# Outer products of the backward chain in 64-row tiles over two head groups, with score gradients in two zero-filled column blocks

## The chip, the cores and the metric

The kernel runs on one core of a Trainium2 chip. The metric is the device time of one launch in microseconds (us); three runs of the kernel before took 2824.84, 2825.89 and 2842.98 us, the median is 2825.89. The engines are named as in the profile: PE is TensorE's matrix multiplication and PEld its weight loads, DVE is VectorE, ACT ScalarE, POOL GpSimd, SP the engine that issues most DMAs (SPq its queue).

## The reference, cut to what matters

One layer and all its gradients. The attention part is recurrent: the sequence of 2048 rows is cut into 64 segments of 32, and 8 memory rows, which are the attention's own output at the segment before, stand ahead of each. There are 32 heads of size 128, the model has 512 columns.

```python
for s in range(n_seg):                                    # 64 segments
    xs = x[:, s * seg_len:(s + 1) * seg_len, :].copy()    # 32 rows
    h = jnp.concatenate([mem, xs], axis=1)                # 8 + 32 = 40 rows
    q = jnp.einsum('btd,dhe->bhte', h, Wq)                # k, v alike
    scores = jnp.einsum('bhqe,bhke->bhqk', q, k) * scale  # then masked
    p = _softmax(scores, axis=-1)
    o = jnp.einsum('bhqk,bhke->bhqe', p, v)
    o = jnp.einsum('bhte,hed->btd', o, Wo)
    mem = o[:, :M, :].copy()                              # M = 8
    outs.append(o[:, M:, :])
```

Beside it stands a feed-forward part with a squared ReLU. The kernel returns the output and the gradients of x, mem0, Wq, Wk, Wv, Wo, w1, b1, w2 and b2. The gradient walks the segments from the last to the first, because each segment's memory gradient is needed by the one before it.

## The kernel before

The program has five parts one after the other: the feed-forward part, the forward chain, the gradients of the memory rows ("left" rows), the backward chain, and the weight gradients. The change lies in the backward chain alone, from B_ORDER to the end of its pool block.

The chain has 64 steps, one for each segment, in 16 blocks of SPB = 4. The 32 heads are four groups (HG = 4) of KH = 8. An SBUF tile holds the 32 rows of a segment for the four groups on its 128 partitions, group g on partitions 32 g to 32 g + 31, and the eight heads of a group beside each other in columns. A step works on two halves p of four heads a group. Its operations, by the names in the table of orders:

- o0mm, o1mm project the incoming gradient with Wo (L390), o0ev, o1ev copy it to gON, o0fl, o1fl transpose it (L167), o0te, o1te copy that to gOT on DVE (L435).
- vp0, vp1 form the value gradients: probabilities (PD) times gON, a product over the segment's rows.
- s0, s1 form the gradients of the probabilities in PSUM (L477). d1 to d4, with the half behind them (d10, d41), turn these on DVE into score gradients gS (L585, L589, L592, L595); tu0, tu1 transpose gS in blocks of 32x32 on DVE into gST (L495).
- kp0, kp1 and qp0, qp1 form the key and query gradients from gS and the queries qN, and from gST and the keys kN. A second matmul adds what the left rows contribute (qNL with GL, kNL with gST).
- ve, vl, ke, kl and qe copy these results out of PSUM, on ACT and DVE (the table ENGS says which); vg, kg and qg multiply them with the turned weights into one sum (L505); ra and rb copy that sum out, ta and tb transpose it (L541), Ha and Hb add it over the groups into the gradient of the step that follows (L550).
- ldp, ldq and ldn load P, qN and kN for the following step through POOL's queue; vtr loads its values transposed through SP's; vc and pb, on POOL, build vT and PD from them; ldv and ldk load the left rows' PGD, gOL, GL and qNL once a block through POOL's queue; ldk0 and ldk1 load kNL once a block through SP's. Names that begin with L. are the left rows' own products (L1284), sums and stores.

vp multiplies all 128 rows at once: for each head number k, the four groups' heads are columns of PD, which is zero outside a group's own 32 partitions, so one matmul of 160 columns (L1417) and one of 64 for the left rows (L1419) serve four heads. kp and qp go through the helper outer (L636), which places each group's matmul on its own 32 rows of the array, four side by side: for each head number, four matmuls of the segment's rows and four of the left rows'.

The order of the work is written by hand. B_ORDER has four rows, for the four places of a step in its block; each "+" behind a name says that the operation belongs to a later step than the row's, so a step begins in one row and ends in the next. Every engine takes its instructions strictly in the order in which the rows issue them, and DMA issues stand in the queue of the engine that issues them.

## Time and profile before

| what | value |
|---|---|
| median of three runs | 2825.89 us |
| the profiled execution's own time | 2830.48 us |
| its span | 2828.7 us, mean granted clock 0.984 |
| the backward chain, 1335 to 2260 us of the span | 925 us: PE busy 842.42, DVE 482.19, ACT 337.09, POOL 362.65 |
| matmuls in that stretch | 22,832 |
| outer products of kp and qp (L636, output b_pp) | 8,192, in sets of four |
| value products (L1417 and L1419) | 512 and 512 |

The page gives busy time of each engine, and an idle engine is no loss unless the work waits for it. In this stretch PE is the engine with least idle time. The view of waits says for each engine what ended its idle time; "issue" there means that nothing the profile shows ended it. A timeline row is the start in us, the duration in us, the engine, line, operation, the tile written and the tiles read, the shapes and the number of instructions drawn together; the duration of a matmul is a modelled one and contains its way through the array, so how fast matmuls follow each other is read from start to start.

### The profile page before, as it was taken

To read this page: it belongs to the slowest core of one execution; us is meant where nothing else is said; L and a number is where in the kernel's file an instruction comes from. 1 tells how busy PE (TensorE), PEld (TensorE's weight loads), DVE (VectorE), ACT (ScalarE), POOL (GpSimd) and SP (SyncE) were. 2 spreads that over 40 slices of the span, in tenths; PEclk is the share of its full clock that TensorE was granted. 3 is DMA by queue.
4 is the path that set the end of the run, shared out by engine and by line. 5 is a ranking of instruction groups with operands and counts; after the bars stand their busy time and mean duration, and the time that the engine had idled before them with its cause. 6 is when DMAs were issued, how large, how long until landed. Compare 5 with 4: busy or idle time off the path is not lost.

```text
span 2828.7 us, 116974 instructions
## 1 busy us (share of the span) xinstructions
PE 2654.5 (94%) x52405; PEld 1449.8 (51%) x52405; DVE 1295.7 (46%) x3819; ACT 976.3 (35%) x2266; POOL 658.9 (23%) x1280
## 2 busy tenths in 40 slices
PE   8999999999999998898998999899899899999999
PEld 3445555555555555455555555555555444444444
DVE  4545656666656664444555555555555401000000
ACT  2324444444444445332333333333333301111111
POOL 1000000000000000123344333343334334322221
PEclk9999999999999999999999999999999999999999
DMA  9764689899989988998577877788777799999992
GB/s 250 274 230 154 165 198 219 205 207 225 220 200 228 210 214 210 260 268 221 152 182 200 208 179 179 184 210 193 175 182 194 228 334 228 216 211 207 201 212 66
DMA packets 842008, 586.76 MB, mean 207 GB/s; under 512 B 638033, under 2 KB 729826, under 8 KB 838178
## 3 DMA queue, kind: packets, MB, share of 16 engines
q1 hardware_dynamic: 800802, 457.86, 70.4%
q0 software_dynamic: 40416, 121.16, 14.1%
q8 instruction: 411, 6.73, 1.0%
q14 instruction: 91, 0.75, 0.1%
q10 hardware_dynamic: 288, 0.26, 0.0%
HBM read 184.95 MB, written 248.79 MB: 153 GB/s over the span
## 4 chain that ended last, share of the span: by engine, by line
PE 47%; issue 3%; DVE 1%; ACT 0%; DMA 0%; POOL 0%; SPq 0%; ACTq 0%; POOLq 0%; DVEq 0%
PE ps_gw L1677 20%; PE ps_gR L505 11%; PE ps_proj L390 4%; PE ps_RL L1284 3%; PE b_pp L636 3%; PE b_T L541 2%; PE ps_tr L167 1%; PE ps_sc L477 1%; PE b_pp L1417 1%; DVE gOT L435 1%; PE ps_R L505 1%; ACT R L432 0%; PE b_pp L1419 0%; DMA b_kNL<-S_NL 0%; PE ps_rows L1588 0%
## 5 line engine op out<-in xcount | busy, mean ns | idle before, releaser
L1677 PE MATMUL ps_gw<-gn,HNc 128*128 128x512 bf16 x1920 | 416.5, 379 | 0.0
L1677 PEld LDWEIGHTS <-HNc 128*128 128x128 bf16 x1920 | 187.9, 98 | 223.8
L432 ACT CAST f_N<-ps_proj 128x512 bf16<-128x512 f32 x320 | 184.1, 581 | 194.8 <-PE ps_proj L390 187.7
L1607 ACT CAST wt<-ps_gw 128x512 bf16<-128x512 f32 x128 | 73.8, 589 | 443.1 <-PE ps_gw L1677 369.3
L390 PEld LDWEIGHTS <-X 128*32 128x32 bf16 x5760 | 144.6, 96 | 135.9 <-DVE X L550 19.8
L1590 DVE TENSOR_TENSOR gx<-ps_rows,gb 128x512 f32<-128x512 f32 x16 | 11.1, 691 | 420.5 <-PE ps_rows L1588 420.5
L896 POOL COPY kM<-f_kT 128x256 bf16<-128x256 bf16 x64 | 25.8, 403 | 749.3 <-DVE f_kT L435 564.1
L505 PE MATMUL ps_gR<-Wv,gv 128*32 128x512 bf16 x2048 | 137.2, 390 | 6.5 <-issue 4.5
L1677 PE MATMUL ps_gw<-GOc,gn 128*128 128x512 bf16 x640 | 139.1, 379 | 1.2 <-DVE gm L1523 1.1
L505 PE MATMUL ps_R<-Wo,OT 128*32 128x256 bf16 x4096 | 128.8, 278 | 6.2 <-issue 5.1
L505 PE MATMUL ps_gR<-Wk,gk 128*32 128x512 bf16 (+1 forms) x2048 | 128.5, 371 | 2.6 <-issue 2.4
L1608 POOL DMA_DIRECT2D out_dram<-wt x120 | 65.0, 543 | 275.8 <-ACT wt L1607 262.0
L390 PE MATMUL ps_proj<-Wo,GT 128*32 128x512 bf16 x2048 | 124.4, 384 | 5.1 <-DVE GT L1329 4.5
L432 ACT CAST gON<-ps_proj 128x512 bf16<-128x512 f32 x128 | 75.0, 586 | 154.7 <-PE ps_proj L390 154.7
L390 PE MATMUL ps_proj<-Wq,X 128*32 128x512 bf16 x1920 | 127.7, 384 | 0.6 <-issue 0.6
L505 PE MATMUL ps_gR<-Wq,gq 128*32 128x512 bf16 (+1 forms) x2048 | 119.9, 350 | 6.7 <-issue 6.6
L390 PE MATMUL ps_proj<-Wk,X 128*32 128x512 bf16 x1920 | 124.9, 384 | 1.1 <-issue 0.4
L390 PE MATMUL ps_proj<-Wv,X 128*32 128x512 bf16 x1920 | 121.5, 378 | 0.2 <-issue 0.2
L1365 POOL COPY PD<-b_P 32x320 bf16<-32x320 bf16 x256 | 115.0, 449 | 17.2 <-DMA b_P<-S_A 6.4
L505 PEld LDWEIGHTS <-OT 128*32 128x32 bf16 x4096 | 105.1, 98 | 14.0 <-issue 7.4
L432 ACT CAST gk<-b_pp 128x256 bf16<-128x256 f32 x128 | 48.1, 376 | 163.4 <-PE b_pp L636 161.3
L505 PEld LDWEIGHTS <-gq 128*32 128x32 bf16 x2816 | 75.4, 98 | 54.0 <-issue 18.8
(290 smaller groups left out, 5271.3 us busy)
## 6 DMA issues: line engine op xcount, KB each, us to landing
S_A<-f_N SPq DMA_DIRECT2D x64, 512.0 KB
out_dram<-wt POOLq DMA_DIRECT2D x134, 128.0 KB, 5.2
S_A<-f_N SPq DMA_DIRECT2D x64, 256.0 KB
S_GB<-gv SPq DMA_DIRECT2D x32, 512.0 KB
S_GB<-gk SPq DMA_DIRECT2D x32, 512.0 KB
S_GB<-gq SPq DMA_DIRECT2D x32, 512.0 KB
b_qN<-S_A POOLq DMA_DIRECT2D x63, 256.0 KB, 3.7
b_kN<-S_A POOLq DMA_DIRECT2D x63, 256.0 KB, 4.9
```

The costliest lines, as they stand in the source:

```text
L167: nc.tensor.transpose(ps_ap, in_ap, ident[base:base + k, base:base + k])
L390: nc.tensor.matmul(o, lhsT=hT[:, dc, :], rhs=x, start=(dc == 0), stop=(dc == DC - 1), tile_position=(0, 32 * g))
L432: nc.scalar.copy(out, in_)
L435: nc.vector.tensor_copy(out, in_)
L505: nc.tensor.matmul(R[32 * g:32 * g + 32, 0:(cs.stop - cs.start) * P].rearrange("p (a b) -> p a b", b=P), lhsT=XT(k, g), rhs=x[:, cs, :], s ...
L541: nc.tensor.transpose(st["T", h][:, 0, c * P:(c + 1) * P], st["R4"][:, (2 * h + c) * P:(2 * h + c + 1) * P], identF[:])
L636: nc.tensor.matmul(o, lhsT=N_[32 * g:32 * g + m, kk * P:(kk + 1) * P], rhs=X(kk)[32 * g:32 * g + m], start=(i == 0), stop=(i == len(jobs) ...
L1284: nc.tensor.matmul(ps["R", i][32 * g:32 * g + 32, :].rearrange("p (a b) -> p a b", b=P), lhsT=B_[n][:, k, g, :], rhs=W(g * KH + k), start= ...
L1365: nc.gpsimd.tensor_copy(PD[32 * g:32 * g + 32, g], C["P"][32 * g:32 * g + 32, :, KW - L:KW])
L1607: nc.scalar.copy(wt[:], ps[:])
L1608: eng(dst, wt[:])
L1677: nc.tensor.matmul(ps[:], lhsT=l(rc), rhs=r(rc), start=(n == 0), stop=(n == RC_ALL - 1))
```

## The change

vp, kp and qp get one helper, halves. For each head number it places two matmuls, on rows 0 to 63 and 64 to 127 of the array, side by side. A half holds two head groups, and the moving operand has two blocks of columns, one for each: a block is zero on the 32 partitions of the other group. So the score gradients gS and the probabilities PD now have the shape [half p, block a, head, column], d4 writes both blocks at once by multiplying with PD (whose zeros make the zeros of gS), and the transposition of gS turns both, with zeros. GLD takes the place of GL, in the same two blocks, filled by four loads a block instead of one; kM takes the place of kNL: a tile that is zero except for the 8 memory rows of the step's place in each group, loaded by four small loads a step (ldm) instead of two loads a block. PSUM is laid out anew: a half of vp has a bank, a half of kp and qp a pair of banks. B_ORDER changes in four ways: ldm stands behind ra in each row, ldk0 and ldk1 are gone, in the second row vea and vg0 stand ahead of kp0, and in the third pb stands behind d41.

Per step kp and qp have 64 matmuls instead of 128 and vp 32 instead of 16. A main matmul of kp has 80 columns instead of 40, of the left rows 32 instead of 16; of qp both have 64 instead of 32; of vp 80 instead of 160 and 32 instead of 64.

```diff
@@ -576,7 +576,7 @@
         for c in range(DC):
             nc.tensor.transpose(ps[:, c * P:(c + 1) * P], XT[:, c].rearrange("p j r -> p (j r)"), identF[:])
-    def ds_ops(o, p, n, sc, Pb, gS, sm):
+    def ds_ops(o, p, n, sc, Pb, gS, sm, last=None):
         t, rr = {}, {}
@@ -592,6 +592,9 @@
             nc.vector.tensor_tensor(out=t[0][:], in0=sc3(sc(), n), in1=bc(rr[0], n), op=ALU.subtract)
         def d4():
+            if last is not None:
+                last(t[0])
+                return
             nc.vector.scalar_tensor_tensor(out=gS()[:, HALF[p], KW - n:KW], in0=t[0][:], scalar=scale,
                                            in1=Pb()[:, HALF[p], :], op0=ALU.mult, op1=ALU.mult)
         o["d1%d" % p], o["d2%d" % p], o["d3%d" % p], o["d4%d" % p] = d1, d2, d3, d4
...
-        "L.G3+ L.I3+ s1+++++ kp0+++++ qp0+++++ d11+++++ vea+++++ d21+++++ vg0+++++ vlb+++++ d31+++++ veb+++++ "
+        "L.G3+ L.I3+ s1+++++ vea+++++ vg0+++++ kp0+++++ qp0+++++ d11+++++ d21+++++ vlb+++++ d31+++++ veb+++++ vg1+++++ "
...
     with sb("bq", 1) as bq, sb("bt", 1) as bt, sb("bs", 2) as bs, sb("be", 1) as be, psum("bpp", 1) as bpp, psum("br", 4) as br:
         G4 = {n: bq.tile([P, HG, KH, SPB, SEG], BF16, name="g" + n) for n in "vkq"}
-        gS = bq.tile([P, KH, KW], BF16, name="gS")
-        nc.vector.memset(gS[:], 0.0)
-
-        PD = be.tile([P, HG, KH, L], BF16, name="PD")
-        PGD = be.tile([P, HG, KH, KW], BF16, name="PGD")
+        gS = bq.tile([P, 2, 2, 4, L], BF16, name="gS")
+        PD = be.tile([P, 2, 2, 4, L], BF16, name="PD")
+        PGD = be.tile([P, 2, KH, KW], BF16, name="PGD")
+        GLD = be.tile([P, 2, KH, KW], BF16, name="GLD")
+        kM = be.tile([P, GW], BF16, name="kM")
         nc.vector.memset(PD[:], 0.0)
         nc.vector.memset(PGD[:], 0.0)
+        nc.vector.memset(GLD[:], 0.0)
+        nc.vector.memset(kM[:], 0.0)
...
         def ldv(b, q=pdma):
             for g in range(HG):
-                q(PGD[32 * g:32 * g + 32, g], S_PL[b][32 * g:32 * g + 32])
+                q(PGD[32 * g:32 * g + 32, g % 2], S_PL[b][32 * g:32 * g + 32])
             q(block(b)["gOL"][:], S_GOL[b])
         def ldk(b, q=pdma):
-            q(block(b)["GL"][:, 0], S_GSL[b])
+            for g in range(HG):
+                q(GLD[32 * g:32 * g + 32, g % 2], S_GSL[b][32 * g:32 * g + 32])
             q(block(b)["qNL"][:], S_NL[b][:, 0, :])
...
             def pb():
                 for g in range(HG):
-                    nc.gpsimd.tensor_copy(PD[32 * g:32 * g + 32, g], C["P"][32 * g:32 * g + 32, :, KW - L:KW])
+                    nc.gpsimd.tensor_copy(PD[32 * g:32 * g + 32, :, g % 2],
+                                          C["P"][32 * g:32 * g + 32, :, KW - L:KW].rearrange("p (h k) n -> p h k n", h=2))
             o["pb"] = pb
             o["ldq"] = lambda q=pdma: q(tile_of("qN", [P, GW])[:], rows[:, GW:2 * GW])
             o["ldn"] = lambda q=pdma: q(tile_of("kN", [P, GW])[:], rows[:, 2 * GW:3 * GW])
-            for p in range(2):
-                o["ldk%d" % p] = lambda p=p: dma(B_["kNL"][:, HC[p]], S_NL[b][:, 1, HC[p]]) if j == SPB - 1 else None
+
+            def ldm():
+                for g in range(HG):
+                    dma(kM[32 * g:32 * g + M], S_NL[b][32 * g + M * j:32 * g + M * j + M, 1, :])
+            o["ldm"] = ldm
...
-                ds_ops(o, p, L, lambda p=p: ps["s", p], lambda: C["P"][:, :, KW - L:KW], lambda: gS, bt)
+
+                def d4(t, p=p):
+                    nc.vector.scalar_tensor_tensor(out=gS[:, p], in0=t[:].unsqueeze(1).to_broadcast([P, 2, 4, L]), scalar=scale,
+                                                   in1=PD[:, p], op0=ALU.mult, op1=ALU.mult)
+                ds_ops(o, p, L, lambda p=p: ps["s", p], lambda: C["P"][:, :, KW - L:KW], None, bt, d4)
                 def tu(p=p):
-                    st[p] = bt.tile([P, 4, 2, 32], BF16, name="gST", tag="gST%d" % p)
-                    turn(st[p], gS, p, j)
+                    st[p] = bt.tile([P, 2, 4, 2, 32], BF16, name="gST", tag="gST%d" % p)
+                    x = gS[:, p]
+                    nc.vector.transpose(st[p][:].rearrange("p a k e q -> p (a k e q)"),
+                                        bass.AP(x.tensor, x.offset, [x.ap[0], [L, 8], [M, 2], [1, SEG]]))
                 o["tu%d" % p] = tu
-                def pair(k):
-
-                    return B_["GL"][:, 0, k, :].rearrange("p (a n) -> p a n", a=2)[:, :, lc]
+                def halves(out, k, jobs):
+                    for i, (X, Y, ends) in enumerate(jobs):
+                        for x in range(2):
+                            r, o = slice(64 * x, 64 * x + 64), out(x)
+                            if ends:
+                                o = o[:, :, 0:2 * M].rearrange("p a (e n) -> p a e n", e=2)
+                            nc.tensor.matmul(o, lhsT=X[r, k * P:(k + 1) * P], rhs=Y(k)[r], start=(i == 0),
+                                             stop=(i == len(jobs) - 1), tile_position=(64 * x, 0), skip_group_check=True)
+
+                def ends_of(T_):
+                    return lambda k: T_[:, :, k, :].rearrange("p a (e n) -> p a e n", e=2)[:, :, :, lc]
                 def vp(p=p):
                     for k in range(4 * p, 4 * p + 4):
-                        o = pp("v")[p][:, k % 4 // 2, k % 2 * 256:k % 2 * 256 + 256].rearrange("p (g n) -> p g n", g=HG)
-                        nc.tensor.matmul(o[:, :, 0:L], lhsT=T["gON"][:, k * P:(k + 1) * P], rhs=PD[:, :, k, :],
-                                         start=True, stop=False, skip_group_check=True)
-                        nc.tensor.matmul(o[:, :, 0:2 * M].rearrange("p g (a n) -> p g a n", a=2),
-                                         lhsT=B_["gOL"][:, k * P:(k + 1) * P],
-                                         rhs=PGD[:, :, k, :].rearrange("p g (a n) -> p g a n", a=2)[:, :, :, lc],
-                                         start=False, stop=True, skip_group_check=True)
+                        halves(lambda x: pp("v")[p][:, x, k % 4 * P:k % 4 * P + P].rearrange("p (a n) -> p a n", a=2)[:, :, 0:L], k,
+                               ((T["gON"], lambda k: PD[:, p, :, k % 4, :], False), (B_["gOL"], ends_of(PGD), True)))
                 def kp(p=p):
-                    outer(pp(p), p, ((KW, L, False, 32, C["qN"], lambda k: gS[:, k, KW - L:KW]),
-                                     (KW, 2 * M, True, 32, B_["qNL"], pair)))
+                    for k in range(4 * p, 4 * p + 4):
+                        halves(lambda x: grads(x, p, "k")[:, :, k % 4, 0:L], k,
+                               ((C["qN"], lambda k: gS[:, p, :, k % 4, :], False), (B_["qNL"], ends_of(GLD), True)))
                 def qp(p=p):
-                    outer(pp(p), p, ((32, 32, False, 32, C["kN"], lambda k: st[p][:, k % 4, 1, :]),
-                                     (32, 32, False, M + M * j, B_["kNL"], lambda k: st[p][:, k % 4, 0, :])), 4 * KW)
+                    for k in range(4 * p, 4 * p + 4):
+                        halves(lambda x: grads(x, p, "q")[:, :, k % 4, :], k,
+                               ((C["kN"], lambda k: st[p][:, :, k % 4, 1, :], False),
+                                (kM, lambda k: st[p][:, :, k % 4, 0, :], False)))
                 o["vp%d" % p], o["kp%d" % p], o["qp%d" % p] = vp, kp, qp
+
+                def grads(x, p, n):
+                    at, w = (0, KW) if n == "k" else (2 * KW, SEG)
+                    return pp(p)[x][:].rearrange("p c (k m) -> p (c k) m", k=2)[:, :, at:at + 2 * w].rearrange(
+                        "p k (a n) -> p a k n", a=2)
+
...
             first["ldq"](dma)
             first["ldn"](dma)
-            first["ldk0"]()
-            first["ldk1"]()
+            first["ldm"]()
             ldk(NB - 1, dma)
...
```

On PE, at the step of B_ORDER's second row, between the last score matmuls of s1 (ps_sc) and the first of kp0 (b_pp). Before:

```order
L477 LDWEIGHTS gOT
L477 MATMUL ps_sc<-b_vT,gOT 32x40
L636 LDWEIGHTS b_qN
L636 MATMUL b_pp<-gS,b_qN 128x40
L636 LDWEIGHTS b_qN
L636 MATMUL b_pp<-gS,b_qN 128x40
```

And now:

```order
L477 LDWEIGHTS gOT
L477 MATMUL ps_sc<-b_vT,gOT 32x40
L505 LDWEIGHTS gv
L505 MATMUL ps_gR<-Wv,gv 32x512
L505 LDWEIGHTS gv
L505 MATMUL ps_gR<-Wv,gv 32x512
```

The sixteen matmuls of vg0 (ps_gR from Wv and gv) have moved from behind qp0 to ahead of kp0.

On SP, from the last stores of a block's gradients (S_GB, S_XG) on, with the transposing loads of vl and of gkL. Before:

```order
L1271 DMA S_GB<-gq 512x1x512
L1370 DMA b_kNL<-S_NL 128x512
L1271 DMA S_GB<-gq 512x1x512
L1370 DMA b_kNL<-S_NL 128x512
L1319 DMA S_XG<-b_XT 128x512
L1271 DMA S_GB<-gk 512x1x512
L1374 DMA_TRANSPOSE b_vl<-S_A 128x8x128 x2
L1307 DMA_TRANSPOSE gNat<-b_gkL 128x8x128
L1259 DMA_TRANSPOSE b_GN<-GT 128x4x128
```

And now:

```order
L1276 DMA S_GB<-gq 512x1x512 x2
L1324 DMA S_XG<-b_XT 128x512
L1276 DMA S_GB<-gk 512x1x512
L1384 DMA_TRANSPOSE b_vl<-S_A 128x8x128 x2
L1312 DMA_TRANSPOSE gNat<-b_gkL 128x8x128
L1379 DMA kM<-S_NL 8x1024 x4
L1264 DMA_TRANSPOSE b_GN<-GT 128x4x128
```

The two loads of kNL are gone, and four loads of kM stand behind the transposing load of gkL.

On POOL, once a block, around the copies that build PD. Before:

```order
L1333 DMA PGD<-S_PL 32x512 x4
L1334 DMA b_gOL<-S_GOL 128x1024
L1365 COPY PD<-b_P 32x320 x4
L1337 DMA b_GL<-S_GSL 128x512
L1338 DMA b_qNL<-S_NL 128x1024
L1367 DMA b_qN<-S_A 128x1024
```

And now:

```order
L1338 DMA PGD<-S_PL 32x512 x4
L1339 DMA b_gOL<-S_GOL 128x1024
L1371 COPY PD<-b_P 32x2x160 x4
L1343 DMA GLD<-S_GSL 32x512 x4
L1344 DMA b_qNL<-S_NL 128x1024
L1374 DMA b_qN<-S_A 128x1024
```

The order is the same; one load of GL has become four of GLD, ahead of the loads of qNL, qN and kN.

35 lines of the change are left out of this document (18 added, 17 removed), and 38 rows, old and new, of the table B_ORDER.

## The prediction

> **What bounds the kernel now.** I read the page first, then the table of stretches, the waits of TensorE, and the timeline of a few steps. The page's head and its instruction queue:
>
> ```profile
> PE 2654.5 (94%) x52405; PEld 1449.8 (51%) x52405; DVE 1295.7 (46%) x3819; ACT 976.3 (35%) x2266; POOL 658.9 (23%) x1280
> ...
> q8 instruction: 411, 6.73, 1.0%
> ```
>
> The stretch of the backward chain (busy time of PE, PEld, DVE, ACT and POOL with their counts, then clock, DMA share and GB/s):
>
> ```profile
> 1335.00:2260.00 925.00, 842.42 (x22832) 475.95 (x22828) 482.19 (x1516) 337.09 (x915) 362.65 (x701) 0.98 0.76 190
> ```
>
> The chain takes 925 us for 64 steps, 14.4 us each, and only code inside it changes. TensorE is busy for 842 of them, VectorE for 482. What TensorE waits for there (total us, times, longest):
>
> ```profile
> PE b_pp L636 <- issue: 38.1, 31, 4.5
> PE ps_gR L505 <- issue: 13.5, 19, 1.2
> PE b_T L541 <- ACT R L432: 5.1, 17, 0.3
> PE ps_sc L477 <- issue: 3.9, 2, 2.0
> PE ps_RL L1284 <- issue: 3.9, 3, 1.7
> ```
>
> So 59.4 us in 55 waits end on "issue", that is on nothing the profile shows, and two thirds of that in the outer products. The longest wait for data has 5.1 us. What "issue" is here, two such waits in a row show:
>
> ```profile
> 1511.39 0.19 PE L636 MATMUL b_pp<-b_GL,b_qNL 32*128 32x16 bf16 x4 [1.37 <-issue]
> ...
> 1511.87 1.05 PE L505 MATMUL ps_gR<-Wv,gv 128*32 128x512 bf16 x16
> 1512.74 1.04 PE L505 MATMUL ps_gR<-Wk,gk 128*32 128x512 bf16 x16
> 1513.71 0.20 PE L636 MATMUL b_pp<-gS,b_qN 32*128 32x40 bf16 x4
> ...
> 1514.00 0.20 PE L636 MATMUL b_pp<-gST,b_kN 32*128 32x32 bf16 x4
> 1515.69 0.19 PE L636 MATMUL b_pp<-gST,b_kNL 32*128 32x32 bf16 x4 [1.49 <-issue]
> ```
>
> Between the waits stand 13 rows of 4 outer products, 32 matmuls of L505 and 11 more rows of 4: 128 matmuls, with their weight loads 256 instructions. Queue q8 moves 6.73 MB in 411 pieces, 16,384 bytes each, and TensorE has 2 x 52,405 records, 255 for each piece. So the waits are those for the next 16 KB of TensorE's own instructions: 256 of them were used up in 2.6 us (1511.39 to 1514.00), and the next piece came 4.30 us after the one before. The bound is TensorE, in places the feeding of its program.
>
> **The change part by part.** Durations are of the profiled execution, 2830.48 us for a span of 2828.7; the runs' median, 2825.89, is 4.6 us lower, and I subtract that at the end.
>
> *Instructions.* Per step kp and qp go from 128 matmuls to 64, vp from 16 to 32: 48 fewer, with loads 96, in 64 steps 6,144.
>
> *Value products (vp).* Before:
>
> ```profile
> 1506.17 0.40 PE L167 MATMUL ps_tr<-ident,gON 128*128 128x128 bf16 x4
> 1506.41 0.23 PE L1417 MATMUL b_pp<-PD,gON 128*128 128x160 bf16 x1
> 1506.48 0.19 PE L1419 MATMUL b_pp<-PGD,b_gOL 128*128 128x64 bf16 x1
> 1506.50 0.23 PE L1417 MATMUL b_pp<-PD,gON 128*128 128x160 bf16 x1
> ...
> 1506.77 0.19 PE L1419 MATMUL b_pp<-PGD,b_gOL 128*128 128x64 bf16 x1
> 1506.80 0.39 PE L167 MATMUL ps_tr<-ident,gON 128*128 128x128 bf16 x4
> ...
> 1507.71 0.19 PE L1419 MATMUL b_pp<-PGD,b_gOL 128*128 128x64 bf16 x1
> 1507.83 0.28 PE L477 MATMUL ps_sc<-b_vT,gOT 128*32 128x40 bf16 x16
> ```
>
> From start to start 160 columns take 0.07 us and 64 take 0.03; eight matmuls 0.39, a step's sixteen 0.78. The key and query products, one half:
>
> ```profile
> 1812.73 0.20 PE L636 MATMUL b_pp<-gS,b_qN 32*128 32x40 bf16 x4
> ...
> 1812.80 0.18 PE L636 MATMUL b_pp<-gS,b_qN 32*128 32x40 bf16 x4
> 1812.82 0.17 PE L636 MATMUL b_pp<-b_GL,b_qNL 32*128 32x16 bf16 x4
> 1812.85 0.18 PE L636 MATMUL b_pp<-gS,b_qN 32*128 32x40 bf16 x4
> ...
> 1812.95 0.21 PE L636 MATMUL b_pp<-gST,b_kN 32*128 32x32 bf16 x4
> ...
> 1813.19 0.20 PE L636 MATMUL b_pp<-gST,b_kNL 24*128 24x32 bf16 x4
> ```
>
> Four matmuls of 32 rows run side by side, and a set of four takes 0.025 us whether it has 40 columns or 16: a floor. In the changed vp a head block has 80 columns (0.035) and 32 (0.025 by that floor), two halves side by side: 0.060, in 8 blocks 0.48. That is 0.30 us a step less, **-19 us**.
>
> *Changes of the array's shape.* From L1419 to the transposes of L167, of the same 128x128 shape, is 0.03 us; to L477, whose output is 32 columns of the array wide, 0.12. Another shape costs 0.09. Once vp has 64 rows, it differs from the transposes on one side of each half, two more changes a step: 0.18 x 64, **+12 us**.
>
> *Key and query products.* kp's half took 0.22 (1812.73 to .95) and takes 4 x 0.060 = 0.24; qp's took 0.27 and takes 8 x 0.028 = 0.22 (64 columns, as L1419). **0**, 3 us either way.
>
> The Trainium skill ("TensorE: Matmul & The Clock Gate", Part 3, The mechanism) says that a weight load overlaps a running matmul only where the row group differs. By it fewer row groups hide less. The trace disagrees: vp's loads, on all 128 rows, are hidden (224 columns in 0.098 us). By it the sum would be that of rival E.
>
> *Instruction waits.* At 2 x 22,832 instructions the stage has 178 pieces, after the change 154. In the stretch above, 96 outer products become 48, so 128 matmuls reach 48 further, mostly into L505 at 0.054 us (1511.87 to 1512.74 for 16): 2.6 + 2.6 = 5.2 us, more than the 4.3 that the piece takes. I let four fifths of L636's 38.1 us go, and a third of the other 21.3, whose pieces hold half a set of outer products less: 22 us in some 24 waits stay. A wait also hides the last matmul's own modelled 0.17 us, 31 fewer times: 37 + 5 = 42, **-42 us**. Bounds: nothing if density is not the cause, -65 if all go.
>
> *VectorE.* d4 writes 320 elements instead of 160, the transposition 512 instead of 256:
>
> ```profile
> L595 DVE SCALAR_TENSOR_TENSOR gS<-ds_t,b_P x128: 314/325/857, 1342.9 to 2240.8; 128x160 bf16<-128x160 f32 x128
> L595 DVE SCALAR_TENSOR_TENSOR l_gS<-ds_t,l_P x32: 424/424/426, 1134.6 to 1325.4; 128x256 bf16<-128x256 f32 x32
> ...
> L495 DVE STREAM_TRANSPOSE gST<-gS x128: 432/445/448, 1343.3 to 2241.2; 128x256 bf16<-128x256 bf16 x128
> ```
>
> 99 ns for 96 elements is 1.03 ns each: +165 ns for d4, and +264 for the transposition (at most +445, if all of it doubles). That is 0.43 us a half, 55 us of work. Where it is late, rows of the timeline show; the first pair is of B_ORDER's third row, the second of its second:
>
> ```profile
> 1839.28 0.45 DVE L495 STREAM_TRANSPOSE gST<-gS 128x256 bf16<-128x256 bf16 x1
> ...
> 1840.00 0.21 PE L636 MATMUL b_pp<-gST,b_kN 32*128 32x32 bf16 x4
> ```
>
> ```profile
> 1883.10 0.45 DVE L495 STREAM_TRANSPOSE gST<-gS 128x256 bf16<-128x256 bf16 x1
> ...
> 1883.39 0.18 PE L636 MATMUL b_pp<-b_GL,b_qNL 32*128 32x16 bf16 x4
> 1883.60 0.20 PE L636 MATMUL b_pp<-gST,b_kN 32*128 32x32 bf16 x4
> ```
>
> Third row: the transposition ends 0.27 before qp0, which will wait 0.2; d11 to d31 and kea0, queued behind it, come 0.5 later, so kg0 waits another 0.2: 0.4. Second row: the end is 0.05 before qp0, TensorE already waits. Here the new order puts vg0 (16 matmuls, 0.87) ahead of kp0; that covers 0.43, but kea0 and tu1 still hold kg0 and qp1: 0.3. For the other two rows I take 0.25 each, between nothing and the third row's 0.4. 1.2 us a block of four steps, 16 blocks: **+19 us** (0 if waits fall together with instruction waits, +35 if the transposition doubles).
>
> *DMAs.* One load of kNL a block becomes four small loads of kM a step, on SP. The narrow place is after the transposition of gkL:
>
> ```profile
> 1806.75 1.30 SPq L1307 DMA_TRANSPOSE gNat<-b_gkL  x1
> ```
>
> ```profile
> L1333 SPq DMA_DIRECT2D PGD<-S_PL x4: 390/418/1029, 1334.3 to 1336.2; - x4
> ...
> DMA to landing us min/median/max: 1.9/3.8/5.4
> ```
>
> SP is free at 1808.05; the fourth issue starts 3 x 0.42 later, at 1809.3, and lands after 3.8, at 1813.1 (the same 32-row loads of PGD, issued by POOL): qp0, at 1812.95, waits 0.15. On POOL, GLD needs four issues for GL's one, 1.3 us by the same row, ahead of the kN load, and pb moves behind d41; that is worth between 0 and 1.3 us a block, and I take 0.15, since no wait of TensorE for kN stands above. Together 0.3 x 16, **+5 us** (0 to 28, with 5.4 to land). qNL, PD and the first memsets cost nothing: same bytes, off the path.
>
> An added wait also lets instructions arrive: 24 of 154 pieces still stall, 16% of 24 us, **-4**.
>
> Sum: -19 + 12 + 0 - 42 + 19 + 5 - 4 = -29. 2830.5 - 29 = 2801.5, at the level of the median **2797 us**.
>
> **The rivals.**
> *B, VectorE stays hidden.* The room in each row is wider than I read and the fetch gain larger: -19 + 12 - 55 = -62 to 2764. For it: VectorE idles 443 of 925 us. Against: the 0.05 us above.
> *C, the instruction waits stay.* They would be set by how busy the DMA rings are (share 0.76), not by density: -42 and -4 go, 2797 + 46 = 2843. For it: 21.3 us sit outside outer products. The Trainium skill ("Runtime: NRT & Kernel Launch", Instruction fetch mechanics) says that crossing a 16 KiB block is mostly hidden; by this rule there was little to gain. The trace has 59.4 us of it.
> *D, kM is late.* The loads queue behind the transposes: at 7.3 us to land, 3.5 more than above, 16 blocks x 3.5 = 56, 2797 + 56 = 2853. It decides from 3.7 us to land on; no row shows 16 KB loads behind a transposition.
> *E, the halves don't overlap* (slower). Two tiles of 64 rows run one after the other, or their loads show. Per step vp, kp and qp cost 0.48 + 0.48 + 0.45 more, 1.4 x 64 = 90, less the 22 us of instruction waits that then vanish: 2797 + 68 = 2865. Against: four tiles of 32 overlap, into as many banks. It decides once overlap is under a third.
>
> **How the numbers follow.** This kernel's measurement tells 1% (28 us) from no change: 2798 and 2854 are the marks. Forecast 0.58, its own range 2775 to 2818, slightly more of it below 2798 (0.31) than above (0.27). B 0.16. C 0.11. D 0.08, half beyond 2854. E 0.07. Faster 0.31 + 0.16 = 0.47; same 0.27 + 0.11 + 0.04 = 0.42; slower 0.04 + 0.07 = 0.11. The range runs from B to C, 2764 to 2845: outside lie D, E and a twentieth below.
>
> **What would show it.** Page: 49,333 matmuls, q8 about 387 pieces. TensorE's issue waits in the chain near 22 us; unchanged means C. L595's successor 0.49 us, the transposition near 0.71. From one 80-column product to the next of its half 0.06 us; 0.12 means E. qp0 waiting on a DMA into kM means D; waits on gST or gk over 30 us, that VectorE was priced too low.

## The result and the profile after

The changed kernel takes 2789.18 us, the median of four runs (2781.49 to 2791.07), against 2825.36 for the kernel before beside it: a ratio of 0.9854, with a 95% interval of 0.981 to 0.9898. That is 36 us less; the prediction had 29 less and 2797. Timed once more beside the first experiments, the pair gave 2803.64 and 2831.53 us, 0.9894 (0.9867 to 0.992), 28 to 30 us less; 2789 had been expected for it. The profiled execution took 2790.5 us, 40 less than that of before, but this pair flatters the change, as the part on the prediction shows.

The page's head and its instruction queue; the stretch of the backward chain (columns as before; in this trace the chain itself runs from 1316 to 2207 us):

```profile
PE 2645.2 (95%) x49333; PEld 1435.7 (51%) x49333; DVE 1346.5 (48%) x3820; ACT 977.0 (35%) x2266; POOL 679.3 (24%) x1325
...
q8 instruction: 387, 6.34, 1.0%
```

```profile
1335.00:2220.00 885.00, 826.54 (x19480) 457.24 (x19476) 525.19 (x1496) 332.72 (x901) 375.15 (x729) 0.99 0.78 193
```

The matmuls and the pieces of instructions are those counted ahead. What TensorE waits for in this stretch (total us, times, longest), the rows that answer to those shown of before and the largest new ones:

```profile
PE b_pp L1432 <- DMA b_kN<-S_A: 13.4, 10, 3.2
PE ps_gR L505 <- issue: 10.3, 10, 1.9
PE b_T L541 <- ACT R L432: 6.0, 18, 0.6
PE ps_sc L477 <- DVE gOT L435: 5.9, 30, 0.5
PE b_pp L1432 <- issue: 3.5, 4, 1.5
PE b_pp L1432 <- ACT gq L432: 2.8, 2, 1.9
PE b_pp L1432 <- DMA kM<-S_NL: 2.0, 6, 0.5
```

"issue" in the outer products has fallen from 38.1 us in 31 waits to 3.5 in 4. At the top now stands a wait for data, the load of the keys kN, which had no row before. A half of the value products, of 0.23 us from the first row to the last where it had 0.36:

```profile
2200.39 0.40 PE L167 MATMUL ps_tr<-ident,gON 128*128 128x128 bf16 x4
2200.72 0.21 PE L1432 MATMUL b_pp<-PD,gON 64*128 64x80 bf16 x2
2200.76 0.19 PE L1432 MATMUL b_pp<-PGD,b_gOL 64*128 64x32 bf16 x2
2200.80 0.20 PE L1432 MATMUL b_pp<-PD,gON 64*128 64x80 bf16 x2
...
2200.86 0.20 PE L1432 MATMUL b_pp<-PD,gON 64*128 64x80 bf16 x2
...
2200.95 0.18 PE L1432 MATMUL b_pp<-PGD,b_gOL 64*128 64x32 bf16 x2
2201.31 0.28 PE L477 MATMUL ps_sc<-b_vT,gOT 128*32 128x40 bf16 x16 [0.18 <-DVE gOT L435]
```

The two halves of the array run side by side (0.06 us from 80 columns to 80). The last row matters too: the scores of TensorE's next lines wait 0.18 us for the copy gOT. This wait is not new: in the trace of before TensorE stands 0.12 us at some 30 such places, which the view of waits leaves out, because it begins at 0.15 us. VectorE's two operations in the two kernels (groups: busy us, mean ns | idle ahead; after first, then before):

```profile
L1422 DVE STREAM_TRANSPOSE gST<-gS 128x512 bf16<-128x512 bf16 x128 | 90.9, 710 | 3.8
L1415 DVE SCALAR_TENSOR_TENSOR gS<-ds_t,PD 128x320 bf16<-128x320 f32 x128 | 63.0, 492 | 7.7
```

```profile
L495 DVE STREAM_TRANSPOSE gST<-gS 128x256 bf16<-128x256 bf16 x128 | 56.8, 444 | 3.8
L595 DVE SCALAR_TENSOR_TENSOR gS<-ds_t,b_P 128x160 bf16<-128x160 f32 x128 | 44.7, 349 | 3.3
```

52 us more of VectorE, for 55 forecast.

**All traces side by side.** I measured the chain from the first product written to b_pp to the last, and summed the view of TensorE's waits between the two (without the first 1.5 us) by what ended them. Before and changed kernel have two traces each. The kernels below the second row are those of the experiments; a ratio is to the runs of before made beside them.

| kernel | ratio (95% interval) | matmuls in the chain | chain us | "issue" us (waits) | VectorE us | DMA us |
|---|---|---|---|---|---|---|
| before | 1 | 22,644 | 906.9; 917.8 | 60.1 (57); 67.9 (56) | 2.2; 2.8 | 0; 0 |
| changed | 0.9854 (0.981 to 0.9898); 0.9894 (0.9867 to 0.992) | 19,572 | 890.9; 886.5 | 14.0 (15); 12.5 (10) | 10.6; 13.4 | 18.7; 14.9 |
| kp and qp in quarters | 1.008 (1.0055 to 1.0106) | 23,668 | 934.9 | 65.3 (52) | 14.1 | 6.0 |
| qp in quarters | 0.9958 (0.9938 to 0.9977) | 21,620 | 909.6 | 43.3 (32) | 13.8 | 5.5 |
| before, vp in halves | 1.0072 (1.0047 to 1.0098) | 23,668 | 918.6 | 61.8 (55) | 13.6 | 1.8 |
| VectorE's addition taken out | 0.9832 (0.98 to 0.9863) | 19,572 | 871.5 | 19.4 (14) | 12.4 | 8.3 |
| transposition twice | 1.0105 (1.0068 to 1.0142) | 19,572 | 947.8 | 10.3 (11) | 72.5 | 9.2 |
| kN first | 0.9862 (0.9836 to 0.9888) | 19,572 | 881.7 | 13.6 (10) | 16.1 | 12.6 |
| all loads first | 0.9816 (0.9778 to 0.9854) | 19,572 | 872.4 | 16.0 (17) | 12.8 | 4.6 |
| vg0 back | 0.991 (0.9876 to 0.9945) | 19,572 | 908.0 | 18.8 (14) | 24.6 | 14.3 |

### The profile page after: what moved, and what is told of

Read it like the earlier page. It is cut to its first block, busy times and chain, and to the rows that moved or that the text cites. A ratio compares the mean times of both kernels' runs of the same rounds, so it can differ in the third digit from the quotient of the medians.

```text
span 2788.7 us, 111417 instructions
## 1 busy us (share of the span) xinstructions
PE 2645.2 (95%) x49333; PEld 1435.7 (51%) x49333; DVE 1346.5 (48%) x3820; ACT 977.0 (35%) x2266; POOL 679.3 (24%) x1325
## 3 DMA queue, kind: packets, MB, share of 16 engines
q0 software_dynamic: 41616, 121.16, 14.2%
## 5 line engine op out<-in xcount | busy, mean ns | idle before, releaser
L505 PE MATMUL ps_gR<-Wv,gv 128*32 128x512 bf16 x2048 | 140.8, 393 | 9.2 <-issue 5.6
L505 PE MATMUL ps_R<-Wo,OT 128*32 128x256 bf16 x4096 | 126.9, 275 | 3.6 <-issue 2.5
L505 PE MATMUL ps_gR<-Wk,gk 128*32 128x512 bf16 (+1 forms) x2048 | 128.4, 376 | 1.9 <-DVE gST L1422 1.1
L505 PE MATMUL ps_gR<-Wq,gq 128*32 128x512 bf16 (+1 forms) x2048 | 111.5, 341 | 4.7 <-issue 4.7
L505 PEld LDWEIGHTS <-OT 128*32 128x32 bf16 x4096 | 104.4, 97 | 10.0 <-issue 4.3
L1703 PEld LDWEIGHTS <-gn 128*128 128x128 bf16 x640 | 62.9, 98 | 76.9 <-issue 3.3
L435 DVE COPY gOT<-ps_tr 128x512 bf16<-128x512 bf16 x128 | 54.3, 424 | 93.9 <-PE ps_tr L167 93.9
```

What stands on the lines that cost most here:

```text
L435: nc.vector.tensor_copy(out, in_)
L505: nc.tensor.matmul(R[32 * g:32 * g + 32, 0:(cs.stop - cs.start) * P].rearrange("p (a b) -> p a b", b=P), lhsT=XT(k, g), rhs=x[:, cs, :], s ...
L1703: nc.tensor.matmul(ps[:], lhsT=l(rc), rhs=r(rc), start=(n == 0), stop=(n == RC_ALL - 1))
```

## The experiments

**Is it the density of instructions? Key and query products in quarters.** Two kernels give the outer products their four tiles of 32 rows back, each tile on its own column block and, as before, its own PSUM bank; all else is that of the changed kernel.

```diff
+                def quarters(p, at, w, jobs):
+                    for k in range(4 * p, 4 * p + 4):
+                        for i, (X, Y, ends) in enumerate(jobs):
+                            for g in range(HG):
+                                r, c = slice(32 * g, 32 * g + 32), at + k % 4 * w
+                                o = pp(p)[g // 2][:, g % 2, c:c + min(w, L)]
+                                if ends:
+                                    o = o[:, 0:2 * M].rearrange("p (e n) -> p e n", e=2)
+                                nc.tensor.matmul(o, lhsT=X[r, k * P:(k + 1) * P], rhs=Y(k)[r, g % 2], start=(i == 0),
+                                                 stop=(i == len(jobs) - 1), tile_position=(32 * g, 0), skip_group_check=True)
-                    for k in range(4 * p, 4 * p + 4):
-                        halves(lambda x: grads(x, p, "k")[:, :, k % 4, 0:L], k,
-                               ((C["qN"], lambda k: gS[:, p, :, k % 4, :], False), (B_["qNL"], ends_of(GLD), True)))
+                    quarters(p, 0, KW, ((C["qN"], lambda k: gS[:, p, :, k % 4, :], False), (B_["qNL"], ends_of(GLD), True)))
-                    for k in range(4 * p, 4 * p + 4):
-                        halves(lambda x: grads(x, p, "q")[:, :, k % 4, :], k,
-                               ((C["kN"], lambda k: st[p][:, :, k % 4, 1, :], False),
-                                (kM, lambda k: st[p][:, :, k % 4, 0, :], False)))
+                    quarters(p, 4 * KW, SEG, ((C["kN"], lambda k: st[p][:, :, k % 4, 1, :], False),
+                                              (kM, lambda k: st[p][:, :, k % 4, 0, :], False)))
```

Both kp and qp:

> Key and query products again in four tiles of 32 rows (128 matmuls a step for 64), all else as in the changed kernel: value products in halves, new VectorE work, new loads. Theory (density of instructions): the streaming time stays, issue waits in the chain return from 14.7 us to about 60, part of the kN waits lies inside them: 2822 to 2832 us. Rival (the waits for instructions went for another cause, such as the new order of the loads): 2785 to 2793 us.

It took 2853.87 us beside 2803.64 for the changed kernel: 50 us more, where 33 to 43 were expected. Its waits:

```profile
PE b_pp L1443 <- issue: 46.1, 34, 2.9
PE ps_gR L505 <- issue: 11.4, 12, 1.9
```

The waits for instructions are back with the matmuls alone, and the rival (another cause, such as the new order of the loads) is out. Query products alone:

> The query products alone in four tiles of 32 rows, the key products in halves: 32 matmuls a step more than the changed kernel, half of the step to the kernel with both in quarters, which stood at 1.008 against 0.989. Theory (density of instructions): issue waits in the chain between the 15 us and the 65 us of the two, some 35 us, ratio 0.996 to 1.001. Rival (a threshold: the piece comes in time until almost all products are in quarters): under 25 us of issue waits, 0.990 to 0.994.

```profile
PE b_pp L1443 <- issue: 17.0, 10, 3.8
PE ps_gR L505 <- issue: 14.2, 12, 2.7
```

Ratio 0.9958 and 43.3 us of issue waits. So they rise with the number of matmuls: 13.3 us (mean of 14.0 and 12.5) at 19,572, 43.3 at 21,620, 65.3 at 23,668. From the first to the last that is 52 us for 4,096 matmuls, which are 32 pieces of instructions: 12.7 ns a matmul, 1.6 us a piece on average. The kernel in the middle lies 4 us above this line, within the 8 us by which the two traces of the kernel before differ, so the threshold of the rival is out; a straight line is not shown more closely than that. The kernel before, with other value products and another order, lies 8 to 16 us above it.

**Value products alone.** The kernel before, with vp, PD and PGD of the changed one, and nothing else:

```diff
-        PD = be.tile([P, HG, KH, L], BF16, name="PD")
-        PGD = be.tile([P, HG, KH, KW], BF16, name="PGD")
+        PD = be.tile([P, 2, 2, 4, L], BF16, name="PD")
+        PGD = be.tile([P, 2, KH, KW], BF16, name="PGD")
...
-                q(PGD[32 * g:32 * g + 32, g], S_PL[b][32 * g:32 * g + 32])
+                q(PGD[32 * g:32 * g + 32, g % 2], S_PL[b][32 * g:32 * g + 32])
...
-                        o = pp("v")[p][:, k % 4 // 2, k % 2 * 256:k % 2 * 256 + 256].rearrange("p (g n) -> p g n", g=HG)
-                        nc.tensor.matmul(o[:, :, 0:L], lhsT=T["gON"][:, k * P:(k + 1) * P], rhs=PD[:, :, k, :],
-                                         start=True, stop=False, skip_group_check=True)
-                        nc.tensor.matmul(o[:, :, 0:2 * M].rearrange("p g (a n) -> p g a n", a=2),
-                                         lhsT=B_["gOL"][:, k * P:(k + 1) * P],
-                                         rhs=PGD[:, :, k, :].rearrange("p g (a n) -> p g a n", a=2)[:, :, :, lc],
-                                         start=False, stop=True, skip_group_check=True)
+                        halves(lambda x: pp("v")[p][:, x, k % 4 * P:k % 4 * P + P].rearrange("p (a n) -> p a n", a=2)[:, :, 0:L], k,
+                               ((T["gON"], lambda k: PD[:, p, :, k % 4, :], False), (B_["gOL"], ends_of(PGD), True)))
```

> The kernel before with the value products alone in halves of 64 rows. The forecast's terms: -19 us of streaming, +12 us for two more changes of the array's shape a step, +4 us for 16 matmuls a step more, which are 8 pieces of instructions more: 2818 to 2826 us against 2825. Rival (the changes of shape hide behind the streaming): 2806 to 2812. Rival (instructions get denser where TensorE has least work for them): over 2832.

2851.46 against 2831.53: 20 us slower, where the forecast's terms gave 3 faster. The time is the one that the second rival gave, but its reason is not seen, as the next lines say. Its waits hold a row that before has only with 0.7 us in 2 waits:

```profile
PE ps_sc L477 <- DVE gOT L435: 6.0, 32, 0.5
PE b_pp L636 <- DVE gS L595: 5.6, 15, 1.5
```

VectorE's work is that of before here, which fits TensorE arriving earlier. In the traces the intervals inside the value products sum to 48.0 us before, 34.2 here, 32.6 in the changed kernel: -14 to -15. The intervals into and out of them sum to 32 us before and 43 in both others, +10: 5.5 us from the transposes, 4.3 to them, and 1.0 to 1.3 to the scores, where the wait for gOT grows from 0.12 to 0.18 us. So by the intervals the halves of vp gain 3 to 5 us; their 1,024 matmuls more would cost 1,024 x 12.7 ns = 13 us by the price above. The issue waits of this one trace (61.8 us) don't show these 13 against the 60.1 and 67.9 of before; 8.1 us of its span lie in a wait for a load of gn behind the chain. Another part stands in the granted clock: its median is 0.981 in the six runs of this kernel and 0.984 in the eleven of before beside them, which over 2840 us is some 8 us by estimate, and in the chain it is 0.972 here, 0.984 and 0.980 in the traces of before. Why it is lower is open. That the value products in halves are a loss by themselves in this kernel is measured; how the 20 us divide is not settled. The reverse, the changed kernel with vp on 128 rows, wasn't run.

**What VectorE's addition costs.** Once taken out (gST is then a fixed tile, whose second half stays zero), once enlarged:

```diff
-                    nc.vector.scalar_tensor_tensor(out=gS[:, p], in0=t[:].unsqueeze(1).to_broadcast([P, 2, 4, L]), scalar=scale,
-                                                   in1=PD[:, p], op0=ALU.mult, op1=ALU.mult)
+                    nc.vector.scalar_tensor_tensor(out=gS[:, p, 0], in0=t[:], scalar=scale,
+                                                   in1=PD[:, p, 0], op0=ALU.mult, op1=ALU.mult)
-                    st[p] = bt.tile([P, 2, 4, 2, 32], BF16, name="gST", tag="gST%d" % p)
+                    st[p] = gST[p]
-                    nc.vector.transpose(st[p][:].rearrange("p a k e q -> p (a k e q)"),
-                                        bass.AP(x.tensor, x.offset, [x.ap[0], [L, 8], [M, 2], [1, SEG]]))
+                    nc.vector.transpose(st[p][:, 0].rearrange("p k e q -> p (k e q)"),
+                                        bass.AP(x.tensor, x.offset, [x.ap[0], [L, 4], [M, 2], [1, SEG]]))
```

> The score gradients and their transposition are made for the first column block alone, so VectorE does 160 and 256 elements again, as before the change; the second block stays at zero, and with it half of the key and query gradients. TensorE's work is unchanged. Forecast's term for VectorE: 19 us (0 to 35) come back, 0.6% of the time: ratio 0.981 to 0.984. From the waits of the changed kernel's trace (VectorE's work named in about 11 us, 6 of them for gOT): 5 to 9 us, 0.986. Rival (VectorE's addition is hidden throughout): 0.989 as the changed kernel.

0.9832, against 0.9894 for the changed kernel: some 17 us less, with intervals that nearly touch (against the first pair's 0.9854 it is 6 us, with intervals that overlap); the chain is 15 to 19 us shorter. The VectorE waits that the view names did not move (12.4 us against 10.6 and 13.4). The load of kN did:

```profile
PE b_pp L1436 <- DMA b_kN<-S_A: 5.8, 8, 2.1
```

With it the waits for DMAs fell by 7 to 10 us: in the changed kernel VectorE's d41 ends later, POOL's copies into PD (pb) wait for it (11.9 us in 16 waits, 5.2 here), and behind pb stand the loads. But the issue waits rose by 5 to 7 us, so the view's waits together hold at most 5 of the 15 to 19 us. The rest stands in stalls too short for the view. From start to start, without the view's waits, the intervals within kp and qp sum to 83.5 us in both traces of the changed kernel, to 69.0 and 69.6 before, and to 68.7 here. The heads of two query products in the changed kernel, of the first half of a step and of the second:

```profile
1601.63 0.20 PE L1432 MATMUL b_pp<-gST,b_kN 64*128 64x64 bf16 x2
1601.73 0.33 PE L1432 MATMUL b_pp<-gST,kM 64*128 64x64 bf16 x2
1601.86 0.26 PE L1432 MATMUL b_pp<-gST,b_kN 64*128 64x64 bf16 x2
...
1605.82 0.19 PE L1432 MATMUL b_pp<-gST,b_kN 64*128 64x64 bf16 x2
1605.85 0.19 PE L1432 MATMUL b_pp<-gST,kM 64*128 64x64 bf16 x2
1605.87 0.19 PE L1432 MATMUL b_pp<-gST,b_kN 64*128 64x64 bf16 x2
```

In the first half the two products with kM start 0.10 us after kN's and take 0.13 to the next set; in the second half 0.03 and 0.02. Nearly every step of the changed kernel has this once. Counting intervals above 0.08 us, such stalls at kM sum to 13.1 and 14.2 us in its two traces, 0.3 and 0.5 before (there at kNL), 4.2 here; those between kp and qp, at gST, to 6.7 and 6.6, 2.4 and 2.5, and 1.0. Late loads are not the reason, since the stalls at kM keep their length (55 of the intervals from kN to kM lie between 0.095 and 0.106 us in one trace) and sum to 13.1 us in the kernel with all loads first, below. In the two kernels with quarters they are 1.6 and 1.2 us. Each of kM's four loads a step has its own semaphore, and these products wait for them; whether that is the cause, no run here tests.

The other direction issues the transposition a second time:

> The transposition of the score gradients is made twice, 0.71 us more of VectorE for each half, 91 us in 128 halves. If VectorE is at the edge as the forecast has it (19 us for 0.43 us a half, where each further microsecond counts in full): over 50 us, ratio above 1.006. If there is still room in some rows: 25 to 45 us. If VectorE is hidden: under 10 us, 0.989 to 0.992.

1.0105, and a chain of 947.8 us: 59 more, for 91 us of added work, so two thirds of it show. This is the theory's first case, VectorE at the edge:

```profile
PE b_pp L1434 <- DVE gST L1424: 58.7, 91, 1.0
PE b_pp L1434 <- ACT b_gkL L432: 10.5, 16, 1.1
```

**The order of the second row undone.** vea and vg0 go back behind kp0 and qp0:

```diff
-        "L.G3+ L.I3+ s1+++++ vea+++++ vg0+++++ kp0+++++ qp0+++++ d11+++++ d21+++++ vlb+++++ d31+++++ veb+++++ vg1+++++ "
+        "L.G3+ L.I3+ s1+++++ kp0+++++ qp0+++++ d11+++++ vea+++++ d21+++++ vg0+++++ vlb+++++ d31+++++ veb+++++ vg1+++++ "
```

> The second row of the order as before the change: kp0 and qp0 right behind the scores, vg0 and vea after them; all else as in the changed kernel. The forecast's reading: vg0 (0.87 us) covers the 0.43 us that VectorE takes longer in this row; without it qp0 waits for gST there, 0.4 to 0.7 us in each of 16 blocks: 7 to 11 us more, ratio 0.990 to 0.993 against 0.985 to 0.989. Rival (the place is covered by other waits): no wait for gST there, within 3 us of the changed kernel.

```profile
PE b_pp L1432 <- DVE gS L1415: 9.7, 16, 1.7
...
PE b_pp L1432 <- DVE gST L1422: 3.9, 16, 0.2
```

Both rows, one wait for each block, are there; the changed kernel has 0.8 and 0.2 us in the outer products for these two. So vg0 covers some 12.6 us of waits, 0.8 a block, which rules out the rival's reason. But most of it is kp0's wait for gS, 0.6 us a block; qp0's for gST, which the forecast named, is 0.2. In the time, 0.991 (0.9876 to 0.9945) can't be told from 0.9894, and the profiled run (2821.9 us) was the slowest of the seven, whose median is 2805.89, so its chain of 908.0 us is not typical.

**The late load of kN.** It is late at one place, in the third row. POOL's queue there in the changed kernel:

```profile
1923.59 1.96 POOL L1371 COPY PD<-b_P 32x320 bf16<-32x320 bf16 x4 [1.31 <-issue]
1925.49 1.97 POOL L1343 DMA_DIRECT2D GLD<-S_GSL  x4
1927.46 0.57 POOL L1344 DMA_DIRECT2D b_qNL<-S_NL  x1
1930.09 0.54 POOL L1374 DMA_DIRECT2D b_qN<-S_A  x1 [2.07 <-issue]
1930.68 1.04 POOL L1389 COPY b_vT<-b_vl 128x1024 bf16<-128x1024 bf16 x1
1931.65 0.40 POOL L1390 COPY b_vT<-b_vTL 128x256 bf16<-128x256 bf16 x1
1932.00 0.54 POOL L1375 DMA_DIRECT2D b_kN<-S_A  x1
```

kN is issued last but P, at 1932.0; qp0 waits for it until 1939.93, 7.9 us later. First, its load alone goes ahead of GLD:

```diff
-        "klb0+++++ L.qst+ qp1+++++ kla0+++++ kla1+++++ L.ldk++ kea1+++++ keb1+++++ qeb1+++++ L.G0++ L.xt+ qg0+++++ "
+        "klb0+++++ L.qst+ qp1+++++ kla0+++++ kla1+++++ ldn+++++ L.ldk++ kea1+++++ keb1+++++ qeb1+++++ L.G0++ L.xt+ qg0+++++ "
...
-        "ldq+++++ Hb+++++ vc+++++ o0mm++++++ o0ev++++++ o1mm++++++ L.H0++ ldn+++++ L.Ko0++ L.Vo0++ xa+++++ o0fl++++++ "
+        "ldq+++++ Hb+++++ vc+++++ o0mm++++++ o0ev++++++ o1mm++++++ L.H0++ L.Ko0++ L.Vo0++ xa+++++ o0fl++++++ "
```

> The load of kN moves ahead of the loads of GLD and qNL on GpSimd's queue in the third row. Theory: kN is late because it is issued behind them and behind the copies of vT; 13.4 us in 10 waits go, and with them some 1.5 us of half clock behind each of the longer ones: 2768 to 2776 us. Rival: kN lands when the DMA queues have room, wherever it is issued: the waits stay, 2789 us. Second rival: the waits go, but TensorE then runs into its next 16 KB of instructions: issue waits rise from 14.7 us, 2783 to 2789 us.

0.9862 beside 0.9894, 2790.9 us beside 2803.64: by the ratios 9 us less and by the times 13, just under the theory's 13 to 21, with intervals that overlap; neither rival's reason is seen. In the trace no wait for kN is left, the issue waits stay at 13.6 us, but the load of qN, whose lateness kN's had covered, has taken its place:

```profile
PE b_pp L1432 <- DMA b_qN<-S_A: 8.6, 6, 2.9
```

The stretches around such a place in this kernel (the last two columns are DMA share and GB/s):

```profile
1864.00:1866.00 2.00, 2.00 (x60) 1.08 (x56) 1.25 (x5) 0.74 (x5) 1.69 (x4) 1.00 0.33 123
1866.00:1868.00 2.00, 2.00 (x44) 1.01 (x40) 1.28 (x7) 0.15 (x1) 2.00 (x5) 1.00 0.43 90
1868.00:1870.00 2.00, 2.00 (x48) 1.33 (x40) 0.58 (x2) 0.58 (x1) 1.96 (x5) 1.00 0.96 334
1870.00:1872.00 2.00, 2.00 (x38) 0.93 (x40) 0.56 (x3) 0.58 (x1) 1.55 (x3) 1.00 0.99 362
```

The DMA engines are less than half used while POOL makes its copies into PD and begins with the loads, and full behind that. So the second kernel issues all loads ahead of these copies:

```diff
-        "d31+++++ L.ldv++ vg1+++++ kea0+++++ keb0+++++ kg0+++++ d41+++++ pb+++++ kp1+++++ tu1+++++ qeb0+++++ qea0+++++ "
-        "klb0+++++ L.qst+ qp1+++++ kla0+++++ kla1+++++ L.ldk++ kea1+++++ keb1+++++ qeb1+++++ L.G0++ L.xt+ qg0+++++ "
+        "d31+++++ L.ldv++ vg1+++++ kea0+++++ keb0+++++ kg0+++++ d41+++++ kp1+++++ tu1+++++ qeb0+++++ qea0+++++ "
+        "klb0+++++ L.qst+ qp1+++++ kla0+++++ kla1+++++ ldq+++++ ldn+++++ L.ldk++ pb+++++ kea1+++++ keb1+++++ qeb1+++++ L.G0++ L.xt+ qg0+++++ "
...
-        "ldq+++++ Hb+++++ vc+++++ o0mm++++++ o0ev++++++ o1mm++++++ L.H0++ ldn+++++ L.Ko0++ L.Vo0++ xa+++++ o0fl++++++ "
+        "Hb+++++ vc+++++ o0mm++++++ o0ev++++++ o1mm++++++ L.H0++ L.Ko0++ L.Vo0++ xa+++++ o0fl++++++ "
```

> In the third row GpSimd issues the loads of qN and kN first, then those of GLD and qNL, and only then makes the copies into PD (pb, which stood ahead of all of them), so all loads but kN and qN are issued 2 us earlier than in the changed kernel, kN 6 and qN 4. Theory (the loads are late because POOL issues them late, at a place where the DMA queues are full 4 us later): the waits for kN (13.4 us) and those for qN that took their place when kN alone was moved (8.6 us) both go: 0.980 to 0.984 of before, 2770 to 2785 us. Rival (the transfers are bounded by bandwidth there, another load is late): within 0.002 of the kernel with kN alone moved, 0.986.

0.9816 (0.9778 to 0.9854), 2774.59 us: the theory's range. No wait of the outer products for kN or qN is left in its view, DMA waits are 4.6 us, and the chain is 872.4 us, 14 to 18 less than the changed kernel's. This version has the lowest median; its interval lies wholly below the changed kernel's second one (0.9867 to 0.992) and overlaps the first.

**The kernel before once more.**

> The kernel before once more, for a second trace of it: 2820 to 2838 us; in the backward chain issue waits near 60 us in some 57 waits and no more than 5 us of waits for VectorE and for DMAs together. If the first trace was an outlier, issue waits under 45 us.

2842.08 us in one run, 4 us above the range expected, a chain of 917.8 us, 67.9 us of issue waits in 56, 2.8 us of waits for VectorE and none for DMAs: the first trace's issue waits were no outlier. The changed kernel, run again beside the first experiments:

> The changed kernel once more, to have its time on the same chip as the next three: 2789 us, 0.985 of before.

2803.64 us and 0.9894, 15 us above what was expected; its interval and the first one's (0.981 to 0.9898) share 0.9867 to 0.9898.

## Why the prediction was right

The forecast's case came: fewer matmuls took most of the instruction waits away, and what VectorE and the loads add gave a good part of it back. That the sum also met the time so closely is in part luck, because terms that it had too small or at nothing nearly cancel. By the means of the two traces each, the chain went from 912.4 to 888.7 us: -24. From start to start of TensorE's matmuls, with the view's waits as parts of their own, this divides into issue waits 64.0 to 13.3, -51; waits for VectorE 2.5 to 12.0, +9.5; for DMAs +16.8; for ACT 5.8 to 9.4, +3.6; value products -17 inside and +5 at their borders; key and query products +14 inside and +4 at their borders; the products of L505 and of the left rows -12 inside; the rest +2. Before rounding that makes the -24. The prediction's -29 was put together otherwise.

*Instruction waits (-42).* Right in mechanism and too small: the waits of the view fell by 51 where the term had 37 of its 42 in them, since 13 us stayed where 22 were left standing. The two kernels with quarters show that more matmuls alone bring them back. The -12 of L505 and the left rows goes with them: the intervals inside these products sum to 284.3 and 51.2 us before, 276.7 and 47.1 after, 284.1 and 49.1 with both products in quarters. Rival C is out. The rule named with it, from the Trainium skill ("Runtime: NRT & Kernel Launch", Instruction fetch mechanics), that crossing a 16 KiB block is mostly hidden, does not hold in this chain: there a piece more costs 1.6 us.

*Value products (-19) and array shapes (+12).* Near enough together: with the waits that stand there -15 inside and +10 at the borders, -5 for -7. The shapes are right (0.152 us instead of 0.056 from the transposes into vp, 0.107 instead of 0.028 out of it). The streaming is -15: four blocks take 0.23 us to the last row, some 0.27 in all, not 0.24. Measured alone in the kernel before, the halves of vp cost 20 us, which no term has.

*Key and query products (0).* The streaming is right, and rival E fell with the 0.06 us between two 80-column products: intervals of at most 0.08 us sum to 59.8 us before and 58.8 after. But the intervals within kp and qp grew by 14 us, through stalls of 0.1 to 0.2 us: 13 us at kM and 4 at gST. The forecast looked for waits that its view would list and had no term for these.

*VectorE (+19).* Right in size by the kernel that takes the addition out (15 to 19 us of chain), and by the one that enlarges it (two thirds of added time show). Rival B is out. The way was only half seen: waits that name VectorE grew by 9.5 us, 5 of them because the wait for gOT passed the view's limit, and most of what comes back without the addition stands in the short stalls of qp, at gST and at kM. That vg0 covers the second row was right: 0.8 us a block without it, though mostly in kp0's wait for gS.

*DMAs (+5).* This is the term that failed. Of its SP half the landing was right: waits for kM are 2.0 us, 2.4 forecast (rival D is out); the 13 us of short stalls at kM's products were not in it. Its POOL half, 0.15 us a block taken from a range of 0 to 1.3, measured 13.4 and 12.4 us, some 0.8 a block. The step took the absence of a wait for kN before as a sign of enough room, and priced at most the 1.3 us of three issues. By the traces, the load in the third row lands 6.7 and 5.6 us after its issue before (medians of a trace) and 7.0 and 7.1 after, so the landing itself hardly changed. What shrank is its lead: it was issued 9.4 and 9.1 us ahead of qp0's first product before, 7.0 and 7.2 after, although qp0 waits for it. So the room was some 2.7 us, and more than 2 us went. How much of that GLD's issues took, how much pb's later place and how much TensorE's shorter step, these runs don't divide; with kN issued 11.7 us ahead (kN first) it lands after 3.1.

So the instructions and the value products saved some 26 us more than forecast, and the waits for VectorE, DMAs and ACT, the short stalls and the borders of kp and qp cost some 30 more: -24 on the chain for -29, errors of both signs that nearly cancel. The runs' -28 to -36 are more than the chain's -24. 3 us more lie between the left rows' last product and the chain's first (13.9 and 12.4 us before, 10.1 and 10.3 after). Ahead of that, in code that the change doesn't touch, the left rows' last product starts at 1326.5 and 1327.7 us in the two traces of before, at 1306.2 and 1325.2 in the changed kernel's, and between 1308.4 and 1324.5 in those of the eight experiments, so both of before stand above all the others. The 20 us by which the first pair of profiles differs there are not explained by these runs; whether some of them belong to the change stays open.

## What to carry to other kernels

Count instructions for each 16 KB piece where matmuls are small: work that keeps its streaming time but halves its matmuls was worth 50 us here, and splitting a fast 128-row product in two for 0.13 us of streaming was a loss in the kernel before. When a queue gets more issues, look at when the loads behind them will run, not only at what the issues cost: the same loads 4 to 6 us earlier, where the DMA queues were less than half used, were worth 14 to 18 us of the chain. And sum the intervals between matmuls from start to start beside the view of waits: 14 us of what this change costs stand in stalls too short for the view, and a wait that seems new may only have passed its limit.

## What the runs showed of the hardware that was not expected

The granted clock halves after waits far shorter than expected. In the changed kernel TensorE waits 1.48 us ahead of 1600.16 us; the stretches behind (the third number from the end is the granted clock):

```profile
1600.16 1.04 PE L505 MATMUL ps_gR<-Wv,gv 128*32 128x512 bf16 x14 [1.48 <-issue]
...
1602.31 1.90 PE L505 MATMUL ps_gR<-Wv,gv 128*32 128x512 bf16 x16
1603.99 1.63 PE L505 MATMUL ps_gR<-Wk,gk 128*32 128x512 bf16 x16
1605.56 0.21 PE L1432 MATMUL b_pp<-gS,b_qN 64*128 64x80 bf16 x2
...
1606.14 1.91 PE L505 MATMUL ps_gR<-Wq,gq 128*32 128x512 bf16 x32
1607.88 0.61 PE L505 MATMUL ps_gR<-Wk,gk 128*32 128x256 bf16 x16
```

```profile
1600.00:1602.00 2.00, 1.75 (x40) 0.97 (x42) 0.04 (x1) 0.00 (x0) 0.00 (x0) 0.95 1.05 384
1602.00:1605.00 3.00, 3.00 (x41) 1.33 (x41) 1.86 (x4) 1.16 (x5) 0.00 (x0) 0.50 0.89 118
1605.00:1608.00 3.00, 3.00 (x84) 1.53 (x79) 1.11 (x4) 0.65 (x2) 1.75 (x4) 0.97 0.17 34
```

For 3 us the clock is 0.50, and 32 matmuls of L505 take 3.25 us (1602.31 to 1605.56) where the next 32 take 1.74 (1606.14 to 1607.88): a wait of 1.5 us costs another 1.5. The same follows the kN wait of 3.25 us that ends at 1939.93. The Trainium skill ("TensorE: Matmul & The Clock Gate", What's actually happening) gives an idle window of about 3.4 us for the fall to half rate; here less than half of that was enough, while other waits of this size and longer (1.36 us ahead of 1385.78, 1.90 ahead of 1772.75) passed without it, so where in a window the wait lies may decide, which no run here tests.

The waits for instructions rise with the number of instructions, on average by 12.7 ns for each matmul and its weight load over a range of 21% in their number, and without a threshold in between.

A matmul whose weights come from a tile loaded anew in each step can start some 0.1 us late although the load is not late: at kM this happened nearly once a step, 13 to 14 us in the chain, and far less (1.2 to 4.2 us) where TensorE's products had four tiles of 32 rows or VectorE less to do. The cause is open.
